# Opening of a fused attention and gMLP kernel: blocks 0 and 1 centred only, loads split anew, blocks 4 to 7 transposed by DMA, second stage in a new order

## The chip, the cores and the metric

The kernel runs on one core of one Trainium2 chip. The metric is the device time of one execution in microseconds, as the median over several runs; lower is better. PE is the matmul engine (PEld its weight loads), DVE the vector engine, ACT the scalar engine, POOL the general engine, and SP the engine that issues most DMAs. SP and ACT each have a DMA queue here.

## The reference

One layer over 2048 tokens of width 512, two branches on the same layer-normed input, summed with the residual:

```python
xn = _layernorm(x, axis=-1)
return x + _A_ref(xn, A_wqkv, A_wo) + _B_ref(xn, B_w_in, B_w_sp, B_b_sp, B_w_out)
```

Branch A is causal attention in a sliding window of 256 tokens, with 32 heads of width 16: `qkv = xn @ wqkv`, softmax of masked scores, times v, times `wo`. Branch B is a gMLP: `z = gelu(xn @ w_in)` of width 1376, split into z1 and z2 of 688 each; z2 is layer-normed along its width; `g = w_sp @ z2 + b_sp` mixes the tokens with a 2048 x 2048 matrix; the result is `(z1 * g) @ w_out`. Gelu is the tanh form. All tensors are bf16; the layer norms have no weights, only a mean and a root.

## The kernel before

Tokens go in 16 blocks of 128. The whole kernel is recorded by hand: an engine executes its instructions in the order in which the Python code emits them, and engines meet only at semaphores.

**First stage** (0 to 84 us of the profile). `load_x` brings x, `w_in` arrives in four pieces, `wqkv` in one. Every block n of x is layer-normed: `ln_stats` on DVE gives mean and variance, `rstd` the root (an addition on DVE, a power on POOL), `ln_apply` writes the normed block `xn` on DVE. `transposes(n, xn)` turns it into `xnT`, in which the width lies along the partitions: for n < 8 by four PE transposes (L282) into a PSUM tile `tp` and an ACT copy (L285), for n >= 8 by a DMA transpose issued by SP (L276). `z_half(n, half)` makes one half of z for one block in eight matmuls (L292, four slices c of the width, two column halves j) and a gelu on ACT (L299); its PSUM tile `zp` has two buffers. `z_stats` and `z_apply` are the layer norm of z2 on DVE. `qkv_unit` makes one 512-wide piece of q, k or v in four matmuls (L129, L147); there are 48 units, listed in `qkv_list`, three or four of them for each block from n = 3 on (`QKV_AT`), and the last four go into the second stage. Before the first data arrive PE multiplies zeros into a tile `heat` (L202, `WARM` times).

The order of PE at the start is: heat, transposes of blocks 0 and 1, z(0,0), z(1,0), z(0,1), transposes of blocks 2 and 3, z(1,1), z(2,0), z(2,1), transposes of 4 and 5, z(3,0), a qkv unit, z(3,1), two qkv units, transposes of 6 and 7, z(4,0), where z(n,h) is half h of block n.

All loads stand at the head of the queues. A DMA carries one of eight semaphores, given in turn, so that from the ninth on its issue waits until the DMA eight places earlier has landed.

**Second stage** (84 to 252 us). The string `ORDER` gives PE's order by hand: `S` a burst of scores (L580) whose exponential ACT computes into E (L589), `m` a mask on DVE (L608), `p` the product of E and v (L523), `n` its normalization on DVE, `q`, `g` and `f` followed by a count that many matmuls of a qkv unit, of the token mixing (`gf`, L443, 16 for a unit, two units for a block of output tokens t) or of the output projections (`fo`, L479 and L486, ten for a unit). A bare number goes on with the unit begun. The block `wspT[t]` of the mixing matrix is loaded by a DMA transpose on SP (L424) into one of two buffers; `load_wsp(t + 2)` is emitted behind the transposed result `uT` of block t (L456), so that it can be issued once block t is through.

## Time and profile before

| | |
|---|---|
| median of 3 runs | 258.57 us (258.11 to 258.86) |
| the profiled execution: time | 258.24 us |
| its span, first to last instruction | 256.4 us |
| PE busy | 249.9 us, 97% |
| ACT busy | 190.7 us, 74% |
| DVE busy | 178.8 us, 70% |
| first z matmul | 7.28 us |
| first matmul of the second stage | 84.03 us |
| last PE matmul starts | 252.29 us |

The times of instructions are counted from the start of the span. 1.84 us of the execution lie outside the span. A matmul's own duration overlaps with that of the next one; where the text counts PE's work it takes the step from one start to the next: 146 ns for a matmul of 344 columns, 216 ns for 512, 56 ns for a transpose of 128. A DMA has landed when the last of its sixteen parts has arrived.

### The profile page before, as it was taken

What the parts mean: (1) busy time and instruction counts of PE and PEld (TensorE: products, weight loads), DVE (VectorE), ACT (ScalarE), POOL (GpSimd) and SP (SyncE); (2) the same over time, 40 slices, a digit from 0 to 9 for tenths busy, and PEclk for the clock granted to TensorE, in tenths of its full rate; (3) what the DMA queues carried; (4) which work ended last, traced back from release to release, by engine and by line L of the source; (5) the groups of instructions that cost most, each with busy time, mean ns of one, the idle gap of its engine ahead of it and who ended that gap; (6) DMA issues with size and microseconds to landing.
All of it is one profiled execution on the core that took longest, in us unless ns stands there. A gap on an engine that the chain in (4) does not pass through costs nothing.

```text
span 256.4 us, 9109 instructions
## 1 busy us (share of the span) xinstructions
PE 249.9 (97%) x4053; PEld 137.4 (54%) x4053; DVE 178.8 (70%) x370; ACT 190.7 (74%) x228; POOL 16.6 (6%) x52
## 2 busy tenths in 40 slices
PE   6999999999999999999999999999999999999993
PEld 2665555555555455464555564556465546465552
DVE  4796997885566758844679857385577877488983
ACT  2777536546546998989898889898988888986800
POOL 4120311211010100000000000000000000000000
PEclk9999999999999999999999999999999999999999
DMA  6994020026201206396843936465469193563032
GB/s 206 393 243 146 0 64 20 0 51 140 58 0 42 66 4 115 72 140 112 153 72 71 187 70 111 93 117 115 41 151 155 48 150 80 117 108 64 20 95 68
DMA packets 65786, 25.38 MB, mean 99 GB/s; under 512 B 53664, under 2 KB 65232, under 8 KB 65744
## 3 DMA queue, kind: packets, MB, share of 16 engines
q1 hardware_dynamic: 64256, 23.74, 44.4%
q10 hardware_dynamic: 1488, 1.03, 1.4%
q8 instruction: 32, 0.52, 0.9%
q14 instruction: 10, 0.08, 0.1%
HBM read 8.41 MB, written 2.10 MB: 41 GB/s over the span
## 4 chain that ended last, share of the span: by engine, by line
PE 96%; DVE 1%; DMA 1%; POOL 0%; issue 0%
PE gf L443 32%; PE zp L292 15%; PE S L580 10%; PE fo L479 9%; PE S L523 8%; PE pj_o L129 6%; PE fo L486 6%; PE pj_f L129 5%; PE pj_f L147 3%; PE pj_o L147 3%; DMA xt<-in_A_x_dram 1%; PE tp L282 1%; DVE stats L240 1%; POOL rs L250 0%; DVE xo L491 0%; DVE xn L268 0%
## 5 line engine op out<-in xcount | busy, mean ns | idle before, releaser
L589 ACT ACTIVATE E<-S 128x1024 bf16<-128x1024 f32 x152 | 141.2, 1025 | 16.1 <-PE S L580 15.8
L443 PE MATMUL gf<-z2n,wspT 128*128 128x344 bf16 x512 | 86.5, 310 | 0.0
L443 PEld LDWEIGHTS <-wspT 128*128 128x128 bf16 x512 | 45.5, 98 | 32.3 <-issue 11.6
L608 DVE TENSOR_TENSOR E<-E,maskFD 128x1024 bf16<-128x1024 bf16 (+2 forms) x48 | 38.4, 808 | 5.9 <-ACT E L589 5.4
L292 PE MATMUL zp<-w_in_sb,xnT 128*128 128x344 bf16 x256 | 41.7, 309 | 0.0
L292 PEld LDWEIGHTS <-xnT 128*128 128x128 bf16 x256 | 24.9, 98 | 15.1
L580 PE MATMUL S<-qpad,kT 32*64 32x512 bf16 (+3 forms) x960 | 31.9, 309 | 0.0
L530 DVE STREAM_TRANSPOSE ot<-S 128x1024 f32<-128x1024 f32 x16 | 19.9, 1244 | 16.7 <-PE S L523 16.5
L449 DVE SCALAR_TENSOR_TENSOR u<-gf,b_all,z 128x344 bf16<-128x344 f32 x32 | 18.3, 571 | 17.9 <-PE gf L443 15.6
L479 PE MATMUL fo<-w_out_sb,uT 128*128 128x512 bf16 (+1 forms) x102 | 24.4, 367 | 0.0
L299 ACT ACTIVATE z<-zp 128x688 bf16<-128x688 f32 x16 | 11.9, 745 | 15.1 <-PE zp L292 15.0
L580 PEld LDWEIGHTS <-kT 32*64 32x64 bf16 x960 | 10.8, 102 | 21.2 <-issue 20.2
L523 PE MATMUL S<-E,v_y 64*32 64x256 bf16 (+2 forms) x960 | 21.8, 231 | 0.0
L523 PE MATMUL S<-E,vx 64*32 64x256 bf16 (+3 forms) x960 | 21.8, 232 | 0.0
L523 PEld LDWEIGHTS <-vx 64*32 64x32 bf16 x960 | 18.4, 90 | 4.1 <-issue 3.7
L523 PEld LDWEIGHTS <-v_y 64*32 64x32 bf16 x960 | 19.2, 90 | 0.6 <-issue 0.6
L299 ACT ACTIVATE z2n<-zp 128x688 bf16<-128x688 f32 x16 | 11.9, 745 | 10.1 <-PE zp L292 10.1
L129 PEld LDWEIGHTS <-wqkv 128*128 128x128 bf16 x128 | 12.5, 98 | 12.4
L129 PE MATMUL pj_o<-xnT,wqkv 128*128 128x512 bf16 x72 | 18.5, 379 | 0.0
L140 DVE TENSOR_SCALAR qpad<-qt,hmask 128x512 bf16<-128x512 bf16 x32 | 9.7, 345 | 11.4 <-ACT qt L138 11.4
L486 PE MATMUL fo<-wo_sb,oT 128*128 128x512 bf16 (+1 forms) x68 | 17.3, 368 | 0.0
L491 DVE TENSOR_TENSOR xo<-fo,xo 128x512 bf16<-128x512 f32 (+1 forms) x17 | 11.1, 654 | 8.4 <-PE fo L486 8.1
(60 smaller groups left out, 197.2 us busy)
## 6 DMA issues: line engine op xcount, KB each, us to landing
xo<-in_A_x_dram SPq DMA_DIRECT2D x16, 128.0 KB, 3.5
out_dram<-xo SPq DMA_DIRECT2D x15, 128.0 KB, 2.2
vx<-v_y SPq DMA_DIRECT2D x16, 102.0 KB, 3.2
xt<-in_A_x_dram SPq DMA_DIRECT2D x3, 512.0 KB, 9.7
wqkv<-in_A_wqkv_dram SPq DMA_DIRECT2D x1, 1536.0 KB, 10.5
w_in_sb<-in_B_w_in_dram ACTq DMA_DIRECT2D x2, 344.0 KB, 5.8
w_in_sb<-in_B_w_in_dram SPq DMA_DIRECT2D x2, 344.0 KB, 6.0
w_out_sb<-in_B_w_out_dram SPq DMA_DIRECT2D x1, 640.0 KB, 5.6
```

What stands on the lines that cost most here:

```text
L129: nc.tensor.matmul(pt[:], lhsT=wqkv[:, c, w0 : w0 + P], rhs=xnT[:, c, t0 : t0 + 512], start=(c == 0), stop=(c == NC - 1),)
L292: nc.tensor.matmul(zp[:, j, 0:HALF], lhsT=xnT[:, c, n * P : (n + 1) * P], rhs=w_in_sb[:, c, f0 : f0 + HALF], start=(c == 0), stop=(c == NC ...
L299: nc.scalar.activation(out=dst.rearrange("p (j f) -> p j f", j=2), in_=zp[:, :, 0:HALF], func=ACT.Gelu_apprx_tanh,)
L443: nc.tensor.matmul(gf[:, 0:HALF], lhsT=wspT[t][:, c, :], rhs=z2n[:, c, j * HALF : (j + 1) * HALF], start=(c == 0), stop=(c == NB - 1),)
L449: nc.vector.scalar_tensor_tensor(out=u[:, j * HALF : (j + 1) * HALF], in0=gf[:, 0:HALF], scalar=b_all[:, t : t + 1], in1=z1[:, t, j * HALF ...
L479: nc.tensor.matmul(fo[:, 0:w], lhsT=uTs[t][:, ch, :], rhs=w_out_sb[:, ch, c0 : c0 + w], start=(ch == 0), stop=False,)
L486: nc.tensor.matmul(fo[:, 0:w], lhsT=oTs[t // 2][:, c, q0 : q0 + P], rhs=wo_sb[:, c, c0 : c0 + w], start=False, stop=(c == NC - 1),)
L523: nc.tensor.matmul(o[32 * s : 32 * s + 32, h, q0 : q0 + ni * KB], lhsT=v, rhs=Et[part, s, e, c0 : c0 + ni * KB], start=(i == 0), stop=(i = ...
L530: nc.vector.transpose(out=ot[:].rearrange("p h b j -> p (h b j)"), in_=o[:].rearrange("p h c -> p (h c)"))
L580: nc.tensor.matmul(o.rearrange("p (e q) -> p e q", e=2)[:, :, c0 - b0 : c0 - b0 + ni * KB], lhsT=kT[32 * s : 32 * s + 32, 2 * g + h, k0 : ...
L589: nc.scalar.activation(out=Et[:, 2 * i : 2 * i + 2, :, b0 : b0 + w].rearrange("p s e q -> p (s e) q"), in_=S[i][:].rearrange("p s (e q) -> ...
L608: nc.vector.tensor_tensor(out=v, in0=v, in1=mask, op=ALU.mult)
```

## The change

Blocks 0 and 1 (`EARLY`) are treated twice. For z they are only centred (`center`, mean subtracted), turned on PE (`turn_early`) into a tile `xcT` of their own, and the root goes in as the scale of gelu, one number for each token, that is for each partition of `zp`. For q, k and v they are normed in full (tile `xq`) and turned by DMA into `xnT`. Block 0 is copied out of PSUM in two pieces, and the transposes of block 1 stand in the middle of z(0,0). Blocks 2 and 3 stay with PE, and blocks 4 to 7 are turned by DMA like the later ones. x0 comes in two halves of 64 rows over both queues, x2 and x3 in one DMA, and `w_in` is split by slices c within a half of the columns. Five late loads are emitted behind the DMA transposes of blocks 0, 1, 4 and 5 (`load_late`). Two v units of the first quarter go ahead of the other qkv units, three heat matmuls fall away, and `ORDER` is another string with the same work in it. Two DMAs of the fallback path, which is not taken here, change their queue.

```diff
-WARM = 11
+WARM = 8
+EARLY = 2
 ORDER = """
-S q4 q4 q4 q2 S 2 g1 m 5 S m 7 S 2 m 1 g6 m S 4 m 5 S 1 g4 p S 5 m 3 n 1 S 3 g7 p S 1 n 2 m 6 S
-f6 S 3 m 1 g5 S 8 m 3 S g10 S 6 p S g1 m 7 S 5 m 3 g2 m S 10 S 4 f4 S 6 g1 S 6 p S 4 m 5 S g9 S
...
+S q4 q4 q4 q1 S 3 m g7 S 2 m 3 S 4 g4 S 7 m 4 m 1 S g3 p S 3 m 6 S 1 m 3 g5 S 9 n 1 p S 1 g7 S 1
+n m 8 g1 S 9 S 2 m 4 f3 S 5 m 1 m S 1 g12 S p 1 m 3 g1 S 10 S 5 g4 m S 3 m 7 S 2 f5 S 4 p S 1 g3
...
+    qkv_list = qkv_list[10:12] + qkv_list[:10] + qkv_list[12:]
...
+        xcT = pa.tile([P, EARLY, NC, P], BF, name="xcT")
...
-        for half in range(2):
-            for k, eng in ((0, nc.sync), (1, nc.scalar)):
-                load_x(eng, 2 * half + k, 2 * half + k + 1)
-                f0 = half * FH + k * HALF
-                eng.dma_start(
-                    out=w_in_sb[:, :, f0 : f0 + HALF], in_=w_in_v[:, :, f0 : f0 + HALF]
-                )
+        def load_w(eng, half, c0, c1):
+            f0 = half * FH
+            eng.dma_start(
+                out=w_in_sb[:, c0:c1, f0 : f0 + FH], in_=w_in_v[:, c0:c1, f0 : f0 + FH]
+            )
+
+        for k, eng in ((0, nc.sync), (1, nc.scalar)):
+            part = slice(k * 64, k * 64 + 64)
+            eng.dma_start(out=xts[0][part, 0, :], in_=x2[part, :])
+        load_w(nc.scalar, 0, 0, 2)
+        load_x(nc.sync, 1, 2)
+        load_w(nc.sync, 0, 2, 4)
+        load_x(nc.scalar, 2, 4)
+        load_w(nc.scalar, 1, 0, 2)
+        load_w(nc.sync, 1, 2, 4)
         load_x(nc.sync, 4, 8)
         nc.sync.dma_start(out=wqkv[:], in_=A_wqkv.rearrange("(c p) f -> p c f", p=P))
-        load_x(nc.sync, 8, 12)
-        load_x(nc.sync, 12, 16)
...
+        def load_late():
+            load_x(nc.sync, 8, 12)
+            load_x(nc.sync, 12, 16)
...
+        def center(n):
+            xc = lt.tile([P, D], BF, name="xc", bufs=EARLY)
+            nc.vector.tensor_scalar(
+                out=xc[:], in0=xts[0][:, n, :], scalar1=mvx[n], scalar2=None,
+                op0=ALU.subtract,
+            )
+            return xc
+
         def transposes(n, xn):
-            if n >= 8:
-                nc.sync.dma_start_transpose(
-                    out=xnT[:, :, n * P : (n + 1) * P], in_=xn[:]
-                )
-                return
+            nc.sync.dma_start_transpose(out=xnT[:, :, n * P : (n + 1) * P], in_=xn[:])
+
+        def turn_early(n, xn, pieces):
             tp = psum["f"].tile([P, NC, P], BF, name="tp", tag="f")
...
+            dst = xcT[:, n] if n < EARLY else xnT[:, :, n * P : (n + 1) * P]
+            k = NC // pieces
+            for c in range(0, NC, k):
+                nc.scalar.copy(out=dst[:, c : c + k, :], in_=tp[:, c : c + k, :])
...
+        def z_half(n, half, inside=None):
+            src = xcT[:, n] if n < EARLY else xnT[:, :, n * P : (n + 1) * P]
             for c in range(NC):
+                if c == NC // 2 and inside is not None:
+                    inside()
...
                 in_=zp[:, :, 0:HALF], func=ACT.Gelu_apprx_tanh,
+                scale=rsx[n] if n < EARLY else 1.0,
...
+        for n in range(EARLY):
+            ln_stats(n, 0, mv0)
+            xcs.append(center(n))
+        turn_early(0, xcs[0], 2)
+        rs0 = rstd(mv0, EARLY)
...
         for _ in ln_batch(2, 2):
             pass
+        for n in range(EARLY):
+            xns[n] = ln_apply(n, "xq")
         for n in (2, 3):
             xns[n] = ln_apply(n)
+        for n in range(EARLY):
+            transposes(n, xns.pop(n))
+        z_half(0, 0, inside=lambda: turn_early(1, xcs[1], 1))
+        z_half(1, 0)
...
                             for k in (4, 5):
-                                xns[k] = ln_apply(k)
+                                transposes(k, ln_apply(k))
+                            load_late()
...
-            if n in (2, 3):
-                for k in (2 * n, 2 * n + 1):
-                    transposes(k, xns.pop(k))
```

More of the change, by code (lines that the diff above doesn't have):

```diff
@@ L60 @@
 ORDER = """
-S q4 q4 q4 q2 S 2 g1 m 5 S m 7 S 2 m 1 g6 m S 4 m 5 S 1 g4 p S 5 m 3 n 1 S 3 g7 p S 1 n 2 m 6 S
-f6 S 3 m 1 g5 S 8 m 3 S g10 S 6 p S g1 m 7 S 5 m 3 g2 m S 10 S 4 f4 S 6 g1 S 6 p S 4 m 5 S g9 S
-m 7 g2 S 5 m 4 n 1 S 4 g6 S n 2 m 4 p S 1 m 3 f3 m S 6 n 1 f2 S p 4 S m 4 g3 S 10 S 1 m 2 g3 n 3
-S 2 m 8 S g6 p S 4 m 2 m 2 S 2 f6 S 2 m 2 g4 S 10 S 2 f7 S p 3 g1 S 1 n 7 S 1 m 4 m m 2 g3 S 10
-S 3 m g7 S 7 p S 2 g6 n S 2 m 6 m 2 S f7 S 3 g5 S m 9 S 2 g5 p S 8 S 2 m 1 g4 n 3 S m 9 S f3 m 3
-n 2 S 2 f5 p S 3 m 2 g1 S 11 m 4 S n p g6 S 2 m 7 S m 1 f6 S 4 g4 S 1 n 4 m 4 S 3 g4 m p S 11 S
-1 f7 S 3 g3 m 3 S 3 m 5 S 2 g1 n 6 p S 9 g1 S 8 m 1 S 3 m 2 m 1 n f1 p S 9 g9 m S 5 n 2 g2 S m 9
-S 5 f5 m 5 p f1 n 9 f10 f10 f10
+S q4 q4 q4 q1 S 3 m g7 S 2 m 3 S 4 g4 S 7 m 4 m 1 S g3 p S 3 m 6 S 1 m 3 g5 S 9 n 1 p S 1 g7 S 1
+n m 8 g1 S 9 S 2 m 4 f3 S 5 m 1 m S 1 g12 S p 1 m 3 g1 S 10 S 5 g4 m S 3 m 7 S 2 f5 S 4 p S 1 g3
+m 4 S 7 n 2 g2 S 8 S 5 m 1 g7 n 1 S 6 m 2 f2 m p S 4 m 2 S 2 f4 S 5 p S 1 m g1 n 6 S 9 g1 S 9 S
+5 m 1 g4 S 10 S m 2 g4 p S 7 n 1 S 1 m 3 m f5 S 3 m 2 g2 m S 10 S 4 g8 S p 6 S 2 f5 S n 5 g3 m S
+9 S 4 g3 m 2 S 7 p S 4 g3 n 1 n 1 S 9 m S 2 f5 m 1 S 4 g1 m 4 S 4 m 1 m 3 p S 3 m f3 n 1 S 6 f1
+S 4 p m S 5 f4 S 6 g3 S n 5 m 3 S 5 g6 m S 6 p S 2 m 2 g6 S 6 m 4 g1 S 12 S n 3 f4 S 2 m 2 p S 2
+g7 n S 2 m 4 m 3 g2 S 12 S m 2 g7 S 9 p S m f6 S 1 m m 3 g3 S 8 n p S 5 f3 n 2 S 5 g1 m 2 S 5 m
+3 S m 5 g16 p f5 n 5 f10 f10 f10
 """
@@ L179 @@
         w_in_v = B_w_in.rearrange("(c p) f -> p c f", p=P)
-        for half in range(2):
-            for k, eng in ((0, nc.sync), (1, nc.scalar)):
-                load_x(eng, 2 * half + k, 2 * half + k + 1)
-                f0 = half * FH + k * HALF
-                eng.dma_start(
-                    out=w_in_sb[:, :, f0 : f0 + HALF], in_=w_in_v[:, :, f0 : f0 + HALF]
-                )
+        def load_w(eng, half, c0, c1):
[12 more added lines that the diff above has]
+        load_w(nc.sync, 1, 2, 4)
         load_x(nc.sync, 4, 8)
         nc.sync.dma_start(out=wqkv[:], in_=A_wqkv.rearrange("(c p) f -> p c f", p=P))
-        load_x(nc.sync, 8, 12)
-        load_x(nc.sync, 12, 16)
-        with nc.allow_non_contiguous_dma(reason="tiny bias gather"):
-            nc.sync.dma_start(out=b_bf[:], in_=B_b_sp.rearrange("(n p) -> p n", p=P))
-        nc.sync.dma_start(out=wo_sb[:], in_=A_wo.rearrange("(c p) n -> p c n", p=P))
-        nc.sync.dma_start(
-            out=w_out_sb[:, 0:5, :], in_=B_w_out[0:640, :].rearrange("(c p) n -> p c n", p=P)
-        )
         idle = pa.tile([P, 512], BF, name="idle")
@@ L212 @@
         )
+        def load_late():
+            load_x(nc.sync, 8, 12)
+            load_x(nc.sync, 12, 16)
+            with nc.allow_non_contiguous_dma(reason="tiny bias gather"):
+                nc.sync.dma_start(out=b_bf[:], in_=B_b_sp.rearrange("(n p) -> p n", p=P))
+            nc.sync.dma_start(out=wo_sb[:], in_=A_wo.rearrange("(c p) n -> p c n", p=P))
+            nc.sync.dma_start(
+                out=w_out_sb[:, 0:5, :], in_=B_w_out[0:640, :].rearrange("(c p) n -> p c n", p=P)
+            )
         def setup_late():
@@ L263, in ln_batch, with ln_apply @@
                 yield
-        def ln_apply(n):
+        def ln_apply(n, name="xn"):
             xs = xts[n // 4][:, n % 4, :]
-            xn = lt.tile([P, D], BF, name="xn")
+            xn = lt.tile([P, D], BF, name=name, bufs=4 if name == "xn" else EARLY)
             nc.vector.tensor_scalar(
@@ L272, in ln_apply @@
             return xn
-        def transposes(n, xn):
-            if n >= 8:
-                nc.sync.dma_start_transpose(
-                    out=xnT[:, :, n * P : (n + 1) * P], in_=xn[:]
-                )
-                return
+        def center(n):
[3 more added lines that the diff above has]
+                op0=ALU.subtract,
+            )
+            return xc
+        def transposes(n, xn):
+            nc.sync.dma_start_transpose(out=xnT[:, :, n * P : (n + 1) * P], in_=xn[:])
+        def turn_early(n, xn, pieces):
             tp = psum["f"].tile([P, NC, P], BF, name="tp", tag="f")
@@ L284, in transposes @@
                 )
-            nc.scalar.copy(out=xnT[:, :, n * P : (n + 1) * P], in_=tp[:])
-        def z_half(n, half):
+            dst = xcT[:, n] if n < EARLY else xnT[:, :, n * P : (n + 1) * P]
[3 more added lines that the diff above has]
+        def z_half(n, half, inside=None):
             zp = ps_s.tile([P, 2, 512], F32, name="zp", tag="S")
+            src = xcT[:, n] if n < EARLY else xnT[:, :, n * P : (n + 1) * P]
             for c in range(NC):
+                if c == NC // 2 and inside is not None:
+                    inside()
                 for j in range(2):
@@ L292, in z_half @@
                     nc.tensor.matmul(
-                        zp[:, j, 0:HALF],
-                        lhsT=xnT[:, c, n * P : (n + 1) * P],
+                        zp[:, j, 0:HALF], lhsT=src[:, c, :],
                         rhs=w_in_sb[:, c, f0 : f0 + HALF],
@@ L325 @@
         xns = {}
-        for b0, k in ((0, 1), (1, 1)):
-            for _ in ln_batch(b0, k):
-                pass
-        for n in range(2):
-            xns[n] = ln_apply(n)
-            transposes(n, xns.pop(n))
+        mv0 = sm.tile([P, 4, 2], F32, name="mvt")
+        xcs = []
+        for n in range(EARLY):
[4 more added lines that the diff above has]
+        for n in range(EARLY):
+            rsx[n] = rs0[:, n : n + 1]
         for _ in ln_batch(2, 2):
             pass
+        for n in range(EARLY):
+            xns[n] = ln_apply(n, "xq")
         for n in (2, 3):
             xns[n] = ln_apply(n)
+        for n in range(EARLY):
+            transposes(n, xns.pop(n))
+        z_half(0, 0, inside=lambda: turn_early(1, xcs[1], 1))
+        z_half(1, 0)
         z_rs = {}
@@ L339 @@
             b, j = divmod(n, 4)
-            if n != 1:
+            if n > 1:
                 z_half(n, 0)
-            if n == 0:
-                z_half(1, 0)
             if n == 4:
@@ L354 @@
                         k = 4 * b + 4 + 2 * (j - 2) + m
-                        xns[k] = ln_apply(k)
-                        if k >= 8:
-                            transposes(k, xns.pop(k))
+                        transposes(k, ln_apply(k))
             if n >= 1:
@@ L370 @@
                 for m in (2, 3):
-                    transposes(m, xns.pop(m))
+                    turn_early(m, xns.pop(m), 1)
             if n % 2 == 1 and n >= 3:
@@ L385 @@
                 nc.vector.tensor_copy(out=b_all[:], in_=b_bf[:])
-            if n in (2, 3):
-                for k in (2 * n, 2 * n + 1):
-                    transposes(k, xns.pop(k))
     ps_s = ctx.enter_context(tc.tile_pool(name="ps_s", bufs=3, space=bass.MemoryType.PSUM))
@@ L740, in attention_with_maximum @@
             xo = cp.tile([P, D], BF, name="xo", bufs=4)
-            nc.sync.dma_start(out=xo[:], in_=x2[bass.ds(row0, P), :])
+            nc.scalar.dma_start(out=xo[:], in_=x2[bass.ds(row0, P), :])
             ws = wspp.tile([P, NB, P], BF, name="wspT")
@@ L779, in attention_with_maximum @@
             nc.vector.tensor_tensor(out=xo[:], in0=fo[:], in1=xo[:], op=ALU.add)
-            nc.sync.dma_start(out=out2[bass.ds(row0, P), :], in_=xo[:])
+            nc.scalar.dma_start(out=out2[bass.ds(row0, P), :], in_=xo[:])
     rows = []
```

## The prediction

> **What bounds the kernel now.** I read the page's busy times first, then the waits of PE, then the chain of waits in order of time, and last the timeline of the first 12 us.

> The page, parts 1 and 4:

> ```profile
> PE 249.9 (97%) x4053; PEld 137.4 (54%) x4053; DVE 178.8 (70%) x370; ACT 190.7 (74%) x228; POOL 16.6 (6%) x52
> ...
> PE 96%; DVE 1%; DMA 1%; POOL 0%; issue 0%
> ```

> PE's own waits (total, times, longest):

> ```profile
> PE tp L282 <- DVE xn L268: 1.4, 2, 0.9
> PE heat L202 <- DVE warm L205: 1.3, 1, 1.3
> ```

> PE waits for nothing after the first transposes: only matmuls taken off PE, an earlier start or a shorter tail help, and nothing that DVE or ACT save in between does. The chain, in order of time (start, length):

> ```profile
> 0.82 2.85 DMA xt<-in_A_x_dram
> 3.69 0.70 DVE stats L240
> 4.79 0.61 DVE stats L240
> 5.87 0.67 POOL rs L250
> 7.44 3.50 PE zp L292 x24
> 10.94 0.45 PE tp L282 x8
> 11.38 3.50 PE zp L292 x24
> 14.88 0.45 PE tp L282 x8
> ...
> 20.25 0.45 PE tp L282 x8
> ```

> From 7.44 us on it is PE alone; the two transpose pieces at 14.88 and 20.25 are blocks 4 to 7. The timeline around blocks 2 and 3:

> ```profile
> 7.17 0.69 DVE L240 BATCH_NORM_STATS2 stats<-xt 128x6 f32<-128x512 bf16 x1 [0.18 <-DMA xt<-in_A_x_dram]
> 9.15 0.70 POOL L250 TENSOR_TENSOR rs<-ve,mhalf 128x2 f32<-128x2 f32 x1 [2.62 <-DVE ve L247]
> 9.89 0.73 DVE L268 TENSOR_SCALAR xn<-xt,mvt,rs 128x512 bf16<-128x512 bf16 x2 [0.81 <-POOL rs L250]
> 10.78 0.61 PE L282 MATMUL tp<-ident,xn 128*128 128x128 bf16 x8
> ```

> Their normed data are ready at 10.62, only 0.16 us before PE wants them. This second chain does not move with block 0.

> **The opening, step by step.** *x0.* Whole blocks (128 KB) landed at 3.67 on SP's queue and 3.48 on ACT's, their first parts at 3.15. Halves: 3.35, between 3.15 and 3.48. *Centring.* Stats and aggregate cost 0.73 + 0.21 to the next start (3.69, 4.42, 4.63). The nearest rows to the new subtraction are qpad's one-operation scaling of the same shape, 0.30 to 0.35, and xn's, 0.40; I take 0.33. Ready at 4.65; the transposes start 0.06 later, at 4.72 against 6.17, since ve, POOL's 0.56 and xn are passed by. *Heat.* The eighth matmul started at 4.22, and steps are 0.216 from there, so eight are out of the way by 4.44; eleven would have lasted to 5.08. *First z.* Four transposes end at 5.11. A full copy takes 0.59 and a half one something between 0.29 and that; I take 0.40. First z matmul 5.61, against 7.28, if the weights are there.

> *The weights.* Each queue carries its bytes in order. Before, 128 + 344 KB on ACT's had landed at 6.01, the same on SP's at 6.45, and the rest (944 KB on each) at 9.13 and 9.30. From 6 to 8 us both together moved 360 GB/s, 0.18 KB per ns for one. By the trace's packets one of 688 bytes took 34 ns, of 1024 45, of 3072 121; the new 1376-byte rows should take about 58, 15% less per byte, worth 0.1 to 0.35 us as they add up. ACT's first weights, 64 KB sooner: 6.01 - 0.36 - 0.15 = 5.5. SP's, behind x1: 6.45 + 0.36 - 0.25 = about 6.5. ACT's last ones, the first half of what z(0,1) needs, stand behind 1008 KB: 9.13 + 0.36 - 0.35 = 9.1.

> *PE from there.* Four z matmuls 5.61 to 6.19, block 1's transposes to 6.42 (its centring is done by 5.84), the other four at 6.54, when SP's weights are in; block 1's copy ends at 7.21, z(1,0) 7.27 to 8.44. Then PE waits 0.7 us for ACT's last weights: z(0,1) 9.17 to 10.34. Blocks 2 and 3 stand behind 664 KB instead of 600 (landed 6.96 and 7.14), so 7.2; the chain to xn takes 3.48 us as before, for the two new xq (0.33 each) fit into DVE's wait for POOL (8.98 to 9.89). Block 3's transposes run at 10.72, and z(1,1) starts at 10.95 against 11.22. So of 1.67 us won at the first z, **0.27** is left. With all landings 0.5 us sooner it is 0.57, with 0.6 later -0.16.

> **Blocks 4 to 7 off PE.** 16 transposes of 55.6 ns: **0.89 us**, all on the path. Their four ACT copies (0.59 each) were not. In exchange SP issues six more DMA transposes; the eight of before took 1.19 to 1.93 us to issue and 2.33 to 4.52 to land. They stand behind wqkv, which landed at 14.42 and should at 14.1. Blocks 0 and 1: about 14.7 and 15.3, wanted by the first q unit at 18.5. Block 4: xn at about 13.7, landed 16.3, wanted by z(4,0) at 20.54 - 1.16 = 19.4; with the slowest landing, 18.2. Waiting for those inputs SP holds back `load_late`: x8 to x11 from 6.03 to about 16.2, landing near 19.5 (from 15.73), first used on DVE at 23.77 before, 22.5 now. Blocks 6 and 7 queue behind b_bf, wo and w_out, whose wo issue took 7.69 us before, until the tiny pieces of b_bf were through; I get 26.5, wanted at 29.2. All hidden; if that cover went, z(4,0) would wait for what it lacks, microsecond for microsecond.

> **The rest at nothing.** The v units first: the same four matmuls of 216 ns; their DVE copies (0.69) have as much room as later ones; wqkv, due at 14.1, is wanted at 15.6. The root as gelu's scale: four gelus (0.745), and ACT idles 0.42 before each. [...] The fallback's queues are not executed.

> **The second stage.** Both strings hold 790 steps of PE: 512 gf, 170 fo, 16 of v, 76 bursts, 16 products. Burst to full matmul occurs 74 times after 73, full to burst 62 after 63, product to burst 13 after 12. With the steps of before (gf to burst 239 ns, burst to gf 331 for the widest) I get **0.09 us** less, nothing. ACT's exponentials start 0.92 us apart, 152 of them 140 us in 168, so in both orders most bursts find their PSUM buffer free by 0.1 to 0.2 us; before, PE never waited. The tail after the last matmul is unchanged.

> Sum: 0.27 + 0.89 + 0.09 = 1.25 us. On the profiled time 258.24 that is 256.99; its median stands 0.33 higher, so 258.57 - 1.25 = **257.3**.

> **Rivals.** *The mixing weights come late (slower).* Between block t = 0's last gf and t = 2's first, the old order has ten fo matmuls beside 32 gf, the new one none: 10.8 us before (94.52 to 105.29), 8.4 now. Before, 3.5 of it passed until the wspT transpose was issued, because a mask and u stood on DVE first; now I count 2.2, leaving 6.2 us, or 4.9 if DVE is as late as before. The sixteen landings took:

> ```profile
> DMA to landing us min/median/max: 4.4/5.6/7.5
> ```

> For t = 2 it was 4.81, so in the forecast PE does not wait, here or at t = 3 (6.4 left). With 7.5 and 4.9, t = 2 waits 2.6 us and t = 3 1.1 or more: 257.3 + 3.7 = 261.0. It decides against the change from 2.0 us of waiting on. For it: the room shrinks by 2.4 us, and both orders are tight. Against: 4.81 is a measured landing at this very place. Chance of that much 0.16.

> *The clock comes up late.* Heat steps are 427 ns until 4.22 us and 216 after, and full clock is granted from 4.20. [...] For: there are three matmuls less. Against: before, PE paused 1.1 and 0.6 us there at full clock. Chance 0.07. [...]

> *The loads give nothing back.* Splitting one queue's bytes otherwise may leave the last weights at 9.7 or later, and x2 and x3 at 7.6: z(1,1) at 11.4, total 257.7 to 258.3. For it: the parts of one DMA lay up to 1.0 us apart (5.01 to 6.01). Against: wider rows. Chance 0.12.

> *The loads run better.* With wider rows all at 390 GB/s from the start, x2 and x3 land at 6.5 and z(1,1) starts at 10.3: 256.6. Chance 0.10.

> **Numbers.** Forecast 0.55 (its own range 256.7 to 257.9), then the rivals. A difference under 0.3% (0.78 us) can't be told from none here. Faster: 0.51 of the forecast, the better loads, 0.02 of the poorer, 0.63 in all. Slower: the late weights, and 0.01 of the late clock: 0.17. Same: 0.04 of the forecast, 0.10 of the poorer loads, 0.06 of the clock: 0.20. Range 256.4 to 259.2: it takes in the late clock, the poorer and nearly all of the better loads, and leaves out the late weights beyond 1.9 us of waiting.

> **What would show it.** First z at 5.6, z(1,1) near 10.95, first burst near 82.9 instead of 84.03, no PE wait over 0.3 us after 11. Wrong if PE waits for wspT near 101 or 110, for xnT at 18.5 or 19.4, if heat-like steps last beyond 4.3, or if the waits before z(0,1) exceed 1.2.

## The result, and the profile after

The changed kernel takes 256.67 us (median of 20 runs, 256.13 to 259.24) against 258.42 us before (20 runs, 257.96 to 259.47): a ratio of 0.9949, 95% interval 0.9932 to 0.9966, or 1.75 us less. The forecast was 1.25 us less. The times before form one group; those after form two: 12 of 20 lie at 256.1 to 256.9 (median 256.55) and 8 at 257.7 to 259.2 (median 258.0).

The profiled execution, 257.66 us with a span of 255.9, belongs to the upper group. Its page, parts 1 and 4 (busy us, share, instructions; then the chain by engine):

```profile
PE 247.8 (97%) x4010; PEld 136.5 (53%) x4034; DVE 177.7 (69%) x371; ACT 189.6 (74%) x225; POOL 16.1 (6%) x51
...
PE 95%; DMA 1%; issue 1%; DVE 1%; ACT 0%; DVEq 0%
```

PE still carries the end, with 19 matmuls fewer (PEld x4034 against 4053). PE's waits (total, times, longest; the rows left out are put down to "issue", at most 0.2 us at a time):

```profile
PE heat L206 <- DVE warm L209: 1.3, 1, 1.3
PE tp L302 <- DVE xc L290: 0.6, 1, 0.6
PE zp L318 <- ACT xcT L308: 0.5, 1, 0.5
...
```

PE has no wait for the mixing weights, for `xnT` or for a load. The chain of waits in the first 14 us (start, length):

```profile
0.80 3.16 DMA xt<-in_A_x_dram
...
4.06 0.70 DVE stats L254
...
5.01 0.36 DVE xc L290
...
5.42 0.62 PE tp L302 x4
...
6.06 0.38 ACT xcT L308
...
6.49 1.33 PE zp L318 x4
7.82 0.43 PE tp L302 x4
8.25 3.70 PE zp L318 x20
11.94 0.45 PE tp L302 x8
```

The root and POOL are gone from the chain, as meant. But the first four z matmuls take 1.33 us (0.76 at full clock, in a run below), and z(1,1) starts at 12.23 us, 1.0 us later than before. The first burst of the second stage is at 84.14 us (before 84.03): in this execution the opening has eaten all that the 16 transposes gave. The last PE matmul starts at 251.82 instead of 252.29. That half microsecond was won in the second stage, which took 167.68 us from first burst to last matmul against 168.26.

So two questions stood open: what the two groups are, and what the new `ORDER` has to do with it.

### The profile page after: what moved, and what is told of

It is laid out like the page before. It is cut to its first block, busy times and chain, and to the rows that moved or that the text cites. A ratio compares the mean times of both kernels' runs of the same rounds, so it can differ in the third digit from the quotient of the medians.

```text
span 255.9 us, 9054 instructions
## 1 busy us (share of the span) xinstructions
PE 247.8 (97%) x4010; PEld 136.5 (53%) x4034; DVE 177.7 (69%) x371; ACT 189.6 (74%) x225; POOL 16.1 (6%) x51
## 4 chain that ended last, share of the span: by engine, by line
PE 95%; DMA 1%; issue 1%; DVE 1%; ACT 0%; DVEq 0%
PE gf L472 32%; PE zp L318 15%; PE S L609 10%; PE fo L508 8%; PE S L552 8%; PE pj_o L131 6%; PE fo L515 5%; PE pj_f L131 4%; PE pj_f L149 3%; PE pj_o L149 2%; DMA xt<-in_A_x_dram 1%; PE tp L302 1%; DVE stats L254 0%; DVE xo L520 0%; ACT xcT L308 0%
## 5 line engine op out<-in xcount | busy, mean ns | idle before, releaser
L472 PEld LDWEIGHTS <-wspT 128*128 128x128 bf16 x512 | 45.7, 98 | 31.6 <-issue 10.6
L318 PE MATMUL zp<-w_in_sb,xnT 128*128 128x344 bf16 x224 | 36.7, 309 | 0.0
L318 PEld LDWEIGHTS <-xnT 128*128 128x128 bf16 x224 | 21.9, 98 | 14.2
L609 PEld LDWEIGHTS <-kT 32*64 32x64 bf16 x960 | 10.8, 102 | 21.2 <-issue 20.1
L552 PE MATMUL S<-E,vx 64*32 64x256 bf16 (+2 forms) x960 | 21.2, 231 | 0.1
L552 PE MATMUL S<-E,v_y 64*32 64x256 bf16 (+2 forms) x960 | 21.2, 231 | 0.0
L324 ACT ACTIVATE z<-zp 128x688 bf16<-128x688 f32 x14 | 10.4, 744 | 14.0 <-PE zp L318 14.0
L131 PE MATMUL pj_o<-xnT,wqkv 128*128 128x512 bf16 x71 | 19.1, 379 | 0.2
L552 PEld LDWEIGHTS <-v_y 64*32 64x32 bf16 x960 | 18.7, 90 | 0.6 <-issue 0.6
L324 ACT ACTIVATE z2n<-zp 128x688 bf16<-128x688 f32 x14 | 10.4, 744 | 9.7 <-PE zp L318 9.7
L515 PE MATMUL fo<-wo_sb,oT 128*128 128x512 bf16 (+1 forms) x65 | 16.5, 367 | 0.3 <-issue 0.3
L264 POOL TENSOR_TENSOR rs<-ve,mhalf 128x2 f32<-128x2 f32 x16 | 11.2, 699 | 70.1 <-DVE ve L261 70.1
```

Of the source, the lines that this page charges most:

```text
L131: nc.tensor.matmul(pt[:], lhsT=wqkv[:, c, w0 : w0 + P], rhs=xnT[:, c, t0 : t0 + 512], start=(c == 0), stop=(c == NC - 1),)
L318: nc.tensor.matmul(zp[:, j, 0:HALF], lhsT=src[:, c, :], rhs=w_in_sb[:, c, f0 : f0 + HALF], start=(c == 0), stop=(c == NC - 1),)
L324: nc.scalar.activation(out=dst.rearrange("p (j f) -> p j f", j=2), in_=zp[:, :, 0:HALF], func=ACT.Gelu_apprx_tanh, scale=rsx[n] if n < EAR ...
L472: nc.tensor.matmul(gf[:, 0:HALF], lhsT=wspT[t][:, c, :], rhs=z2n[:, c, j * HALF : (j + 1) * HALF], start=(c == 0), stop=(c == NB - 1),)
L515: nc.tensor.matmul(fo[:, 0:w], lhsT=oTs[t // 2][:, c, q0 : q0 + P], rhs=wo_sb[:, c, c0 : c0 + w], start=False, stop=(c == NC - 1),)
L552: nc.tensor.matmul(o[32 * s : 32 * s + 32, h, q0 : q0 + ni * KB], lhsT=v, rhs=Et[part, s, e, c0 : c0 + ni * KB], start=(i == 0), stop=(i = ...
```

## Experiments on the clock

**The changed kernel again.** No edit.

> The changed kernel once more, unchanged. Theory A (the clock's rise is what splits its times into a group near 256.5 and one near 258.0): executions fall into the same two groups again; if the profiled one is of the lower group, its granted clock is full from about 4.2 us and not from 9.7, and z(1,1) starts near 11.3, 0.9 us sooner than the 12.23 of the first profile. Theory B (late landings of x0, x1 and the weights split the times): a profile of the lower group shows x0 landed by 3.5 and x1 by 5 instead of 3.96 and 5.95, with the same late rise of the clock.

256.67 us (6 runs, 256.11 to 257.97, ratio 0.9946, 0.9928 to 0.9963), again in two groups, four and two. The profiled one, 257.97, is of the upper group, and again the clock record, in which the trace keeps from when on full clock was granted, begins late, at 10.05 us (9.71 in the first, 4.20 before). The loads were better than in the first (x1 at 5.36 us against 5.95), so late loads alone do not make the upper group. An execution of the lower group was not profiled.

**Eleven heat matmuls.**

```diff
-WARM = 8
+WARM = 11
```

> The changed kernel with 11 heat matmuls instead of 8. Theory A (clock): at half clock the heat lasts to about 5.95 instead of 4.65, so PE is busy until the first transposes and the clock rises by 7 us in every execution; the group near 258 vanishes, the median is 256.5 to 256.8, the spread under 0.8 us; transposes of block 0 start up to 0.6 us later where the rise comes late. Theory B (landings): still two groups 1.5 us apart, and a median equal or up to 0.3 us worse.

256.52 us (5 runs, 256.30 to 256.99, ratio 0.994, 0.9927 to 0.9952). The upper group is gone. PE's timeline:

```profile
1.25 3.88 PE L206 MATMUL heat<-idle 128*128 128x512 bf16 x11 [1.25 <-DVE warm L209]
4.98 0.39 PE L302 MATMUL tp<-ident,xc 128*128 128x128 bf16 x4
5.83 0.76 PE L318 MATMUL zp<-w_in_sb,xcT 128*128 128x344 bf16 x4 [0.47 <-ACT xcT L308]
6.99 0.40 PE L302 MATMUL tp<-ident,xc 128*128 128x128 bf16 x4 [0.40 <-DVE xc L290]
7.25 3.32 PE L318 MATMUL zp<-w_in_sb,xcT 128*128 128x344 bf16 x20
10.41 0.61 PE L302 MATMUL tp<-ident,xn 128*128 128x128 bf16 x8
10.85 1.33 PE L318 MATMUL zp<-w_in_sb,xcT 128*128 128x344 bf16 x8
```

Full clock came at 4.00 us, four z matmuls take 0.76, z(1,1) starts at 10.85 and the first burst at 82.77, 1.37 us before that of the changed kernel's profile; the two groups of times lie 1.46 apart. A second set of five runs gave 257.0 us (256.29 to 257.09; ratio 0.9957, 0.9944 to 0.9969):

> The changed kernel with 11 heat matmuls once more, beside the run with fillers on the same chip: 256.5 us, in one group between 256.2 and 257.1.

Ten runs, then, and none above 257.1, where the changed kernel has 10 of 26 at 257.7 or more. In the profiles of kernels with eleven heat matmuls or as long a heat the clock rose at 4.0, 4.2, 4.3, 4.8, 5.0, 5.4, 5.6, 6.1, 6.2, 7.1 and 7.2 us; with eight at 9.71 and 10.05. From this rise to its fall behind the last matmul, full clock lasted 245.76, 249.17, 252.59 or 256.00 us in the fourteen profiles (252.59 before the change, 245.76 in the first profile after it), each time a whole number (72 to 75) of stretches of 3.413 us. One such stretch ahead of their rise, at 6.29 and 6.64 us, the two late profiles did not yet have full clock; with nine heat matmuls and two more behind block 0's transposes (the next run) it rose at 6.41, and in two kernels with as long a heat as eleven at 6.14 and 6.17. What is different with eight is that the heat is over by 4.85 us, and that pauses of 0.6 and 0.5 us follow it (PE's waits above). What sets the moment of the rise these runs do not show.

That the late clock makes the upper group is thus shown in two profiles of that group and by its going with the longer heat; that all ten slow executions had a late clock is inferred from their times.

**Heat in the pause.** Nine ahead of block 0's transposes, two behind them.

```diff
-WARM = 8
+WARM = 9
...
         turn_early(0, xcs[0], 2)
+        for _ in range(2):
+            nc.tensor.matmul(heat[:], lhsT=idle[:, 0:P], rhs=idle[:], start=True, stop=True)
```

> The changed kernel with 9 heat matmuls ahead of block 0's transposes and 2 more behind them, in PE's wait for the copy of block 0: 11 in all, so PE has as many instructions as in the run with 11, which had no waits in the products. [...] Rival: nine are too few, as eight were, and some executions get the clock at 9.7 and more: a second group near 257.8.

256.75 us (10 runs, 256.11 to 258.28, ratio 0.9951, 0.9936 to 0.9966): nine at 256.1 to 257.3, one at 258.28. In the profile z(1,1) starts at 10.83 although the clock rose only at 6.41 us. It is not measurably better than the changed kernel or than eleven. No version here beats the changed kernel's median by more than the intervals; eleven only take the upper group away.

## Experiments on the second stage

**Blocks 4 to 7 by DMA alone**, with the loads behind them; opening, heat and `ORDER` of before.

```diff
         def transposes(n, xn):
-            if n >= 8:
+            if n >= 4:
...
-                                xns[k] = ln_apply(k)
+                                transposes(k, ln_apply(k))
+                            load_late()
```

> The kernel before with one part of the change alone: blocks 4 to 7 turned by DMA, the five late loads emitted behind the transposes of blocks 4 and 5. Theory A (16 transposes of 56 ns came straight off PE's path): 0.89 us less than before, 257.5, and the first burst of scores at 83.1 instead of 84.0. Rival (the transposes land too late behind wqkv or b_bf, or the moved loads do): PE waits before z(4,0) or z(6,0), and the gain is under 0.4 us or negative.

264.09 us (261.62 to 265.29; ratio 1.0226, 1.0188 to 1.0264). The first stage won what was forecast: first burst at 83.17 us, 0.86 before that of the kernel before. The second stage lost 6.3. One row of PE's waits is new, and four places in PE's timeline make it up:

```profile
PE S L521 <- issue: 5.5, 4, 1.7
```

```profile
111.50 0.25 PE L521 MATMUL S<-E,vx 64*32 64x192 bf16 x1
113.33 0.21 PE L521 MATMUL S<-E,vx 64*32 64x128 bf16 x1 [1.44 <-issue]
...
127.18 0.21 PE L521 MATMUL S<-E,v_y 64*32 64x128 bf16 x1 [1.73 <-issue]
...
140.68 0.24 PE L521 MATMUL S<-E,vx 64*32 64x192 bf16 x1 [1.53 <-issue]
...
204.15 0.21 PE L521 MATMUL S<-E,v_y 64*32 64x128 bf16 x1 [0.76 <-issue]
```

PE stops in the middle of a product, and no semaphore, no tile and no other engine is named. What fits these stops stands in the page's list of DMA queues:

```profile
q8 instruction: 32, 0.52, 0.9%
```

These are 32 packets of 16 KB. PE executes 4053 weight loads and 4053 products in the kernel before, 8106 instructions or 31.7 pieces of 256, so by number the packets fit PE's own instructions, one for each piece, and they come while it runs: in the kernel before the first starts at 17.3 us and the last at 255.1. Counted in PE's program, the four stops stand ahead of instructions 1987, 2499, 3011 and 5827, each 195 more than a multiple of 256. A matmul is two PE instructions (weights, product), and by the trace's weight loads the stops are 256, 256 and 1408 matmuls apart, each a multiple of 128. A product `p` is 128 matmuls in 1.2 us (two of the sixteen have 64), a whole piece, while 256 instructions of mixing take 18.7 us. By these numbers I read the stops so: where a product falls so that a piece is used up in a few microseconds, PE is at the next boundary before the next packet, which takes 0.9 to 1.6 us in the kernel before, is there.

**The new ORDER alone** on the kernel before: the string of the changed kernel, nothing else.

> The kernel before with the new order of the second stage alone. Theory A (in the profile of the changed kernel the second stage, from the first burst to the last matmul, took 167.7 us against 168.3, most of it in the products of E and v, 20.2 against 20.8): 0.5 us less than before, near 257.9. Rival (that was one profile's chance; by the steps alone the orders differ by 0.09): within 0.2 us of before. Rival 2 (mixing weights late): 0.5 us or more slower, with a wait before the first gf of t = 2 or 3.

259.34 us (258.98 to 259.56; ratio 1.0043, 1.003 to 1.0056). The row `PE S L580 <- issue: 1.1, 2, 0.7`; steps of 0.98 and 0.74 us at 197.69 and 237.92, at instructions 5827 and 7619, again 195 and a multiple of 256. Each of these two parts alone is slower than no change.

Two readings were left. *The pieces*: each order must fit PE's instruction count, since every instruction taken out of the first stage (16 transposes, 32 instructions) moves the boundaries against the second stage. Or *the timing*: the transposes and late loads disturb the old order, the new order suits the new opening. The next three runs tell them apart.

**The same as blocks 4 to 7 by DMA, with PE's count restored**: as long a heat, in 27 pieces instead of 11.

```diff
-WARM = 11
+WARM = 27
...
-            nc.tensor.matmul(heat[:], lhsT=idle[:, 0:P], rhs=idle[:], start=True, stop=True)
+            nc.tensor.matmul(
+                heat[:, 0:208], lhsT=idle[:, 0:P], rhs=idle[:, 0:208], start=True, stop=True
+            )
```

> The kernel before with blocks 4 to 7 turned by DMA and the late loads behind them, as in the earlier run that took 264.1 us, but with 27 heat matmuls of 208 columns in place of 11 of 512. The heat lasts as long; it only gives back the 16 matmuls (32 PE instructions) that the transposes took out, so that each instruction of the second stage stands at the place in PE's program that it has in the kernel before. Theory A, PE's instructions come in pieces of 256, and the old order starves where a whole product lies in one piece: the waits of 1.0 to 2.0 us in four products are gone, no PE wait over 0.5 us after 84 us, and the time is that of before less the 16 transposes, 258.3 - 0.9 = 257.4 us. Theory B, the moved loads and transposes or an earlier second stage disturb the old order: the same waits are there, 263 to 265 us.

257.83 us (257.31 to 258.26; ratio 0.9986, 0.9977 to 0.9994), 6.3 us less by heat matmuls that compute nothing. All of PE's waits:

```profile
PE heat L194 <- DVE warm L199: 1.3, 1, 1.3
PE fo L479 <- issue: 0.6, 4, 0.2
PE tp L286 <- DVE xn L272: 0.4, 1, 0.4
PE fo L486 <- issue: 0.3, 2, 0.2
PE pj_f L147 <- issue: 0.2, 1, 0.2
```

The row of 5.5 us is gone; spans of 261.85 and 255.27 differ by 6.58, the four long steps had summed to 6.55. The time of 257.4 was missed by 0.4, and this lies outside the span: by the medians 2.4 us lie there, and 1.7 in the kernel before, while the span is 1.0 us shorter. The trace has one instruction packet more, 8 KB where the 32 above have 16, at 257.24 us, 2.0 after the last instruction. The run with the stops has it too, the other kernels do not. The changed kernel moves two DMAs of the unused fallback from SP to ACT and so shortens SP's program; that this keeps the packet away was not tried.

**The changed kernel with the count of before**: the same edit on it (27 heat matmuls of 208 columns).

> The changed kernel with 27 heat matmuls of 208 columns in place of 8 of 512 (as long a heat as 11 of 512, so the clock should come up at 4 us as in the run with 11). PE then has as many instructions as in the kernel before, and the new order stands where it stood in the run of the old opening with the new order, which lost 0.98 and 0.74 us at two products. Theory A (pieces of 256 instructions): PE waits of 0.7 to 1.0 us at about 196 and 236 us, time 257.3 to 258.2 us, that is 0.8 to 1.7 over the 256.5 of the changed kernel with 11 heat matmuls. Theory B (the new order suits the new opening's timing, whatever the count): no such waits, 256.5 us.

258.32 us (12 runs, 257.0 to 259.28; ratio 0.9999, 0.9985 to 1.0013), 1.8 over the run with eleven heat matmuls. The stop is back, once, at the place where the new order alone had had one:

```profile
197.38 0.31 PE L611 MATMUL S<-qpad,kT 32*64 32x256 bf16 x6
198.80 0.40 PE L611 MATMUL S<-qpad,kT 32*64 32x256 bf16 x10 [1.11 <-issue]
```

It is instruction 5827 again, a step of 1.41 us; the other place passed this time. In the profile 0.83 more had gone in the opening (ACT's last weights at 9.53, clock at 5.6 us).

**The old order in the changed kernel**, with eleven heat matmuls.

> The changed kernel with 11 heat matmuls of 512 columns and the old string ORDER. Theory A (pieces of 256 instructions): old order and PE count are those of the run that took 264.1 us, so the same four products wait for their instructions; with the better opening 262 to 264 us, and the new order is a necessary part of the change. Theory B (the order does nothing, as the prediction had it, 0.09 us): 256.6 us.

262.79 us (262.63 to 264.19; ratio 1.0189, 1.0169 to 1.0209):

```profile
PE S L552 <- issue: 4.3, 4, 1.9
```

The same four instructions as with the old opening (1987, 2499, 3011, 5827), steps of 0.85, 2.11, 1.49 and 0.93 us. So PE's count decides, and not the opening's timing: old order and short count stop four times with either opening; old order and old count do not (the two kernels with the opening alone, below, are held for 0.55 us at the most); the new order stops with the old count and not with the short one. In the eleven stops of 0.74 us and more, PE goes on 1.28 to 1.72 us after the end of the piece's packet; at the other boundaries of the second stage, in every profile, at least 1.44 us had passed. The packets take 0.9 to 2.0 us and start between 3.4 us before PE enters the piece ahead and 3.4 after it. What makes one start late was not settled.

## Experiments on the opening alone

**The opening alone**: the changed opening with eleven heat matmuls, `ORDER` of before, blocks 4 to 7 turned on PE, PE's count as before.

```diff
         def transposes(n, xn):
+            if 4 <= n < 8:
+                xns[n] = xn
+                return
...
+            if n in (2, 3):
+                for k in (2 * n, 2 * n + 1):
+                    turn_early(k, xns.pop(k), 1)
```

> The changed opening alone: the changed kernel with 11 heat matmuls, the old ORDER, and blocks 4 to 7 turned on PE as in the kernel before, so that PE has as many instructions as in the kernel before and the old order stands where it stood. This isolates the first term of the prediction. Theory A: no waits in the products, z(1,1) near 10.9 us (before 11.22), and the time 0.3 to 0.5 us under before: 257.8 to 258.0 us. If the opening is worth nothing without the rest, 258.3 us; if the late loads and two DMA transposes disturb the second stage, over 259 us.

258.86 us (258.44 to 259.48; ratio 1.0026, 1.0017 to 1.0035): a miss. No stop in the products, z(1,1) at 11.24 with the clock at 5.04 us, and then a wait that no other kernel has:

```profile
20.12 0.39 PE L305 MATMUL tp<-ident,xn 128*128 128x128 bf16 x4
21.26 0.38 PE L305 MATMUL tp<-ident,xn 128*128 128x128 bf16 x4 [0.76 <-DVE v_y L154]
```

The transposes of blocks 6 and 7 take their PSUM buffer from a pool that the qkv units use too, and with v first it is DVE's copy of a v unit that block 7 waits for.

**The opening alone, q units first as before:** as above, without the line that puts two v units ahead.

> The changed opening alone once more (11 heat matmuls, old ORDER, blocks 4 to 7 turned on PE, PE's count as in the kernel before), but with the qkv units in the old order too. With v units first, block 4's transposes waited 0.8 us at 20.3 for a PSUM buffer that the v unit's copy on DVE still held. If that is what cost the opening its gain: that wait is gone, first burst at 83.6 to 84.2 us, and the time 257.6 to 258.4, that is 0.5 to 1.2 under the 258.9 with v first, less what PE waits at 16 us for blocks 0 and 1. If not, 258.9 again.

258.20 us (257.76 to 259.0) against 258.12; ratio 1.0003, 0.9994 to 1.0011. The wait is gone, 0.7 us came back, and nothing is left of the opening's gain. The profiled execution, 259.0, is the slowest of the eleven: in it the clock rose at 7.2 us, z(1,1) started at 11.56, and one product of the second stage was held for 0.55 us, at the boundary at 5827.

**Eleven heat matmuls, q units first**, in the changed kernel.

```diff
-    qkv_list = qkv_list[10:12] + qkv_list[:10] + qkv_list[12:]
```

> The changed kernel with 11 heat matmuls and the qkv units in the order of the kernel before, q of the first quarter ahead of v. The prediction had the v units first at nothing. If that edit serves only to give blocks 0 and 1 time (a q unit reads blocks 0 to 3 of xnT, a v unit block 0 alone... the first unit runs at 15.5 us, and the DMA transposes of blocks 0 and 1 land at 15.3 to 17.3): PE waits for them 0 to 1.8 us at 15.5, time 256.5 to 258.3. If the landing is hidden all the same, 256.5.

257.04 us (256.63 to 257.38; ratio 0.9959, 0.9946 to 0.9972): no wait for blocks 0 and 1, whose transposes had landed at 15.02 and 15.65 when the first unit started at 15.83. Beside the 257.0 of eleven heat matmuls on the same chip, v first is worth nothing here; it costs 0.7 us where blocks 6 and 7 use PE. (The two v units put first are units 10 and 11, which read blocks 2 and 3 and not block 0.)

## Why the prediction was right, and where it was not

*Sign and size.* 257.3 was forecast and 256.67 measured, inside the range of 256.4 to 259.2; faster had the largest chance. The nearest profile to the lower group is that of eleven heat matmuls: 1.26 us at the first burst (82.77 against 84.03) and 0.49 in the second stage, 1.75 in all; the forecast had 1.16 and 0.09. That the sum came so near is in part luck. The second stage gave more than forecast, the clock took some of it back, and that the new order fits the shorter count of instructions, which is worth 6.3 us (262.79 against 256.52 with eleven heat matmuls), was in no term. In the first profile one of the prediction's own signs of being wrong stood as well: steps at half clock lasted to 9.71 us, beyond 4.3, and the first burst came at 84.14 instead of 82.9.

*Blocks 4 to 7, 0.89 us: right.* 0.86 at the first burst with this edit alone. The cover held, though some landings were mis-sized: block 4 at 16.25 (16.3 forecast), x8 to x11 at 22.2 (19.5), blocks 6 and 7 at 29.6 and 30.1 (26.5). Block 6 had been forecast 2.7 us ahead of its use at 29.2; it came 0.9 ahead of z(6,0) in the first profile (30.5) and 0.18 ahead with eleven heat matmuls (28.95 and 29.13). PE waited for neither, but almost all of this cover was gone.

*The opening, 0.27 us: a sum with the wrong condition.* With the clock early z(1,1) started at 10.85 (10.95 forecast), 0.37 won; with a late one it was 12.23, 1.0 lost. Alone, even with eleven heat matmuls, the opening gave 0.00. Its worth differs by execution: in six profiles of the changed kernel with about as much heat as eleven, whatever else was changed, the first burst was at 82.62 to 83.60 us, 1.41 to 0.43 before that of the kernel before; if 0.89 of it is always the blocks, 0.52 down to -0.46 are left for the opening, by this estimate. Its steps were mis-sized too. In the first profile (in brackets, with eleven heat matmuls) the halves of x0 landed by 3.96 (3.35) instead of 3.35, x1 at 5.95 (5.61) instead of 4.45, SP's first weights at 7.5 (7.2) instead of 6.5, while the half copy was as taken (0.43 us from its start to the first z matmul). The first four loads took 0.56 to 0.81 us each to issue where those before took 0.40 to 0.45, and this I had not counted. At full clock little of it reached z(1,1): x1 put off block 1's transposes (6.99 in the run with eleven, done by 6.42 in the forecast) and z(1,0) to 8.06, and so used up the 0.7 us that PE was to wait for ACT's last weights; z(0,1) started at 9.24, and 9.17 had been forecast.

*The late clock: foreseen, with a wrong chance.* It had 0.07 and came, by the times, in 10 of 26 executions. The pauses that I held against it (PE paused at full clock before too) prove nothing, for those came after the rise at 4.20 us. How long half clock lasts after a late rise, and so the place of this rival in the range, no run had shown; in the runs the rise came 5.5 and 5.9 us later than before, and the groups lie 1.46 us apart. The 0.7 us that PE was to wait for the last weights could hide none of it, since they had gone to the late x1, and z(0,1) started at 10.6 in the profile, long after its weights (9.31). With the gain of the second stage such executions end at 258.0, about 0.4 under before.

*The second stage, 0.09 us: mis-sized, and for a reason that the sum could not hold.* The count of steps was right, but steps have no fixed price. With no stops at all it took 168.26 (before) and 168.16 us (old order, count restored), and 167.66 to 167.91 with the new order and the short count in six profiles: 0.25 to 0.6 less. In the first two profiles nearly all of it lies within the products, 18.41 us before and 17.85 after, summed from a product's first matmul to its last: of the fourteen with 128 matmuls, seven were 0.05 to 0.18 over the usual 1.18 before, and three by 0.02 to 0.11 after. What these small steps are was not settled. And the same term had hidden a loss of six microseconds: the order was costed as if it could be judged without the count of instructions ahead of it.

*The root as gelu's scale: at nothing, as forecast.* The gelus of z by form (ns min, median, max):

```profile
L324 ACT ACTIVATE z<-zp x14: 744/744/746, 14.8 to 79.6; 128x688 bf16<-128x688 f32 x14
...
L324 ACT ACTIVATE z<-zp,rs x2: 834/834/835, 9.5 to 10.8; 128x688 bf16<-128x688 f32 x2
```

90 ns more for a gelu with a scale per partition (834 against 744). PE waited for none of them.

*The mixing weights late (0.16): did not happen.* No run has a PE wait for `wspT`. Of the better loads, x2 and x3 came in time (6.13 us in the second run with eleven heat matmuls, 6.5 in that rival), but z(1,1) started at 10.70 there, sooner than in any other profile, and not at 10.3: PE was only then through z(0,1), which had started at 9.09, and the transposes. The poorer loads happened in part: in the run of the changed kernel with the count of before the last weights came at 9.69 and z(1,1) at 11.69.

## What to carry to other kernels

PE is busy to 97% here, and 32 of its instructions taken out of the first stage cost the old order 6.3 us in the second (264.09 against 257.83 with 16 idle matmuls in their place). Each of the two orders held for one count only. So after an edit that changes the count, look for waits put down to "issue" inside runs of short instructions, and try a few idle matmuls more or fewer before blaming the edit. Parts of a change can then each be slower than nothing (264.09 and 259.34 against 258.42) and still be faster together (256.67). And a warm-up can be long enough in most executions and not in all: with eight heat matmuls 10 of 26 times were 257.7 us or more, with eleven none of ten was above 257.1. Look at the single times for two groups before trusting one profile.
